# A fused attention and two-layer MLP kernel: all weight groups of the last layer converted first, their stores issued from SyncE, and one more x made on GpSimd

## The chip, the cores and the metric

One core of one Trainium2 chip runs the whole program. The time is the device time of one execution in microseconds (us); the kernel before takes 877.24 us (median of 3 runs, 876.63 to 878.43). A profile is taken of one further execution.

## The reference

Three stages follow each other. The inputs are float64 where they are weights of the two MLP layers, float32 else.

```python
phi(x): proj = x @ w_phi;  proj -= max|proj|;  return [exp(proj), exp(-proj)]
kv = phi(k)^T v;  attn = (phi(q) kv) / (phi(q) sum(phi(k)) + 1e-6)    # 4 batches x 8 heads x 576 x 64
x  = attn as 2304 tokens x 512
h  = max(max(x @ w1, x @ w2), x @ w3);  y = h @ w_out                   # d_ff 768
z  = y @ w_in;  g = max(z, 0) + alpha * min(z, 0);  out = g @ w_out2    # d_ff 2048
```

## The kernel before, in words

Two heads form a pair; the 16 pairs are worked on one after the other (line 453): queries of the pair before (`queries`, line 335) beside keys of this one (`keys`, line 267). Most products are done in three matmuls of a high and a low half (`three`, line 260).

**A pair's x.** At the end of `queries` the numerators stand in `nd[0]`; the denominators go through DRAM: `dc<-nd` (line 388), reciprocal on VectorE, `r_d<-dc` (line 393), and back, spread over partitions, as `xr<-r_d` (line 400). These DMAs are issued from GpSimd. Lines 401 to 408 then make x for each half of the 576 tokens: a product (line 402), its high half (line 405 on GpSimd, or `hi_act`, line 64, on ScalarE), and the low half, a subtraction (line 70). The choice `e` is GpSimd for the first three pairs and VectorE for all others.

**The first layer** (`layer1`, line 422) is called 48 times: 4 batches x 2 token halves x 6 groups of 128 columns. One call, a *unit* here, is 36 matmuls into three PSUM tiles `p` (line 265), which ScalarE (line 436) and VectorE (lines 437 and 439) read; GpSimd stores the result `ho` as `h_d` (line 441). Units start once batch 0 has its four x, from the fifth pair on; 14 of the 48 stand after the loop over pairs (line 623). Units of the loop share three PSUM banks, so that a bank is wanted again by the next unit.

**Weights of the later layers** come as float64 and are made into a float32 word (`words`, line 502, with `from_f64`, line 72) by two instructions on ScalarE (lines 77, 80) and two on VectorE (lines 84, 86). One such *conversion* takes a staged tile `st` (three buffers) that SyncE loads three ahead (`stage`, line 490: the next load is issued when a conversion is through), and yields a word `wt` (eight buffers). Three kinds of conversion stand in the list `todo`:
- `do_quarters` (line 529): the four column groups of `w_out2`, each 4 conversions, combined into seven words by four VectorE instructions (line 514) and *parked*, that is stored to DRAM as `q_d` (line 526), 28 stores in all; they are read back late, in the third layer (line 758).
- `do_out` (line 523): 6 conversions of `w_out`, split into high and low halves `wo`, wanted when the second layer begins (line 675).
- `do_quad` (line 555): four groups of `w_in`, each 4 conversions and 7 splits `wi`, wanted in the third stage (line 773).

That makes 38 conversions in 58 steps. After each unit behind the loop, steps are taken from the list, with low priority (line 626); in the second layer three steps after each token chunk (line 694).

**Order.** A scheduler that works with priorities and a simulated timeline writes each engine's order; engines then run in that order, and each waits in order for what it needs. So an edit in one place can change the order of hundreds of instructions elsewhere.

Of the kernel before, what the change touches and what calls it, by code (L numbers as in the profile page):

```python
# [23 lines left out]
NPAIR = H // 2  # L24
# [23 lines left out]
def tile_kernel(ctx: ExitStack, tc: tile.TileContext, qT, kT, tails, v, w_phi, w1, w2, w3, w_out, w_in, w_out2, alpha, out):  # L48
# [11 lines left out]
    nc = tc.nc  # L60
    V, A, G = nc.vector, nc.scalar, nc.gpsimd

    def hi_act(dst, src):
        A.activation(dst, src, AF.Copy)  # L64
# [4 lines left out]
    def sub(eng, dst, src, hi):  # L69
        eng.tensor_tensor(dst, src, hi.bitcast(F32), op=ALU.subtract)  # L70
# [36 lines left out]
    q_d = dram.tile([4, 7, P, 512], F32, name="q_d")  # L107

    def bank(tag, bufs, nm):
        return ps.tile([P, 512], F32, tag=tag, bufs=bufs, name=nm)  # L110
# [8 lines left out]
    def at(shape, dtype, name, tag=None, bufs=1):  # L119
        pool = ap if (tag or name) in KEYS_ONLY else lp  # L120
        return pool.tile(shape, dtype, name=name, tag=tag or name, bufs=bufs)
# [34 lines left out]
    def i_of(pair):  # L156
        return pair[0] * NPAIR + pair[1]

    def plain_kv(pair):
        return pair[0] < 2  # L160
# [57 lines left out]
    def project_queries(pair):  # L218
        ops = features(pair, "q")
        for g, tiles in enumerate(GROUPS):  # L220
            pp = at([P, 4, P], F32, tag="pp", bufs=2, name="pp")
            less_max(*project(ops, tiles), pp)
            yield g, tiles, pp
# [39 lines left out]
    def products(dst, ops, **kw):  # L263
        for i, (x, y) in enumerate(ops):
            nc.tensor.matmul(dst, x, y, start=i == 0, stop=i == len(ops) - 1, **kw)  # L265
# [69 lines left out]
    def queries(pair):  # L335

        parts = ("q",) if plain_kv(pair) else ("qh", "ql")
        qf = []
        for n, (o, w) in enumerate(CHUNKS):
            qf.append([])  # L340
            for x in parts:
                tag = f"qh{n}" if x != "ql" and pair[1] % 2 * len(x) != 1 else f"ql{n}"
                qf[n].append(at([P, 2, 2, w], F32 if plain_kv(pair) else F32R, tag=tag, bufs=1, name=x))
        nd = [at([P, S], F32, tag="nd", bufs=3, name="nd") for _ in range(2)]

        def num(n):
            o, w = CHUNKS[n]
            kv = kvs_of[pair]
            for h in range(2):
                pn = bank("p1", 3, "pn") if pair[0] == 0 else bank("pn", 1, "pn")  # L350
                ops = []
                for s in range(2):
                    q_ = [t[:, h, s] for t in qf[n]]
                    k_ = [t[:, h, s] for t in kv]
                    ops += [(k_[0], x) for x in q_] + [(x, q_[0]) for x in k_[1:]]
                products(pn[:, :w], ops)
                A.activation(nd[h][:, o : o + w], pn[:, :w], AF.Copy)

        def tail():
            yield 2, (0,), tail_of[pair]  # L360

        for g, tiles, pp in chain(project_queries(pair), tail()):
            o, w = (0, 2 * P, SM)[g], ST if g == 2 else 2 * P
            pt = bank("pn" if pair[0] == 0 and g == 1 else "pt", 1, "pt")
            for i in range(len(tiles)):
                for h in range(2):
                    c = h * len(tiles) * P + i * P
                    nc.tensor.transpose(pt[:, c : c + P], pp[:, 2 * i + h], ident)  # L368
            n = min(g, 1)
            dst = [t[:, :, :, o - CHUNKS[n][0] : o - CHUNKS[n][0] + w] for t in qf[n]]  # L370
            if plain_kv(pair):
                e = dst[0]
            else:
                e = at([P, 2, 2, 256], F32, tag="qe", bufs=2, name="qe")[:, :, :, :w]
            pv = pt[:, : 256 * len(tiles)].rearrange("p (h s) -> p h s", h=2)[:, :, -w:]
            A.activation(e[:, :, 0], pv, AF.Exp)
            A.activation(e[:, :, 1], pv, AF.Exp, scale=-1.0)
            if not plain_kv(pair):
                (hi_dve if g == 1 else hi_act)(dst[0], e)
                sub(V, dst[1], e, dst[0])  # L380
            yield
            if g != 1:
                num(n)
        yield
        dc = at([P, S // D], F32, tag="dc", bufs=2, name="dc")
        for h in range(2):
            dr = D * (1 - h)
            nc.gpsimd.dma_start(dc[h * D : (h + 1) * D], nd[h][dr : dr + 1].rearrange("a (p n) -> a p n", p=D))
        nc.gpsimd.dma_start(nd[0][D:], nd[1][D:])
        V.tensor_scalar(dc, dc, EPS, None, op0=ALU.add)  # L390
        V.reciprocal(dc, dc)
        rows = r_d[pair[0], pair[1]]
        nc.gpsimd.dma_start(rows.rearrange("h (p n) -> (h p) n", p=D), dc)
        res = []
        for c in range(2):
            cs = slice(c * CH, (c + 1) * CH)
            xr = raw_tile()
            for h in range(2):
                r = slice(h * D, (h + 1) * D)
                nc.gpsimd.dma_start(xr[r], rows[h : h + 1, cs].to_broadcast([D, CH]))  # L400
            e = G if i_of(pair) < NPAIR - 1 else V
            e.tensor_tensor(xr, nd[0][:, cs], xr, op=ALU.mult)
            xh, xl = x_tiles(c)
            if e is G:
                G.tensor_copy(xh, xr)
            else:
                hi_act(xh, xr)
            sub(e, xl, xr, xh)
            res.append((xh, xl))
        xs[pair[0]].append(res)  # L410

    def raw_tile():
        return xs_.tile([P, CH], F32, tag="xr", bufs=3, name="xr")

    def x_tiles(half):
        t = x_tile(half)
        return t[:, 0], t[:, 1]
# [65 lines left out]
    def granule(pool, nm):  # L483

        return pool.tile([P, 2, 512], F32R, tag="w", name=nm)
# [13 lines left out]
    def word():  # L499
        return sp.tile([P, 512], F32, tag="wt", bufs=8, name="wt")  # L500

    def words():

        wt = word()
        run(from_f64(staged.pop(0), wt))
        stage()
        return wt

    def split(dst, src):
        hi_act(dst[:, 0], src)  # L510
        sub(V, dst[:, 1], src, dst[:, 0])

    def both(dst, x, y, op=ALU.subtract):
        V.tensor_tensor(dst, x, y, op=op)  # L514
        return dst
# [3 lines left out]
    def split_out(k):  # L519
        wo[k] = granule(ring2, "wo")  # L520
        split(wo[k], words())

    def do_out():
        return [lambda k=k: split_out(k) for k in range(NF1)], [w_out[k] for k in range(NF1)]

    def park(p, i, x):
        nc.gpsimd.dma_start(q_d[p, i], x)

    def do_quarters(p):
        b = {}  # L530
# [24 lines left out]
    def do_quad(q):  # L555
        x = {}
        wi[q] = {}

        def get(n):
            x[n] = words()  # L560

        def to(i, n):
            pool = ring2 if (q == 0 and i < 4) or (q == 3 and i > 0) else ring
            wi[q][i] = granule(pool, "wi")
            split(wi[q][i], x[n])

        def second():
            get("22")
            x["s1"] = both(word(), x["21"], x["22"], ALU.add)

        def third():
            get("11")
            x["s2"] = both(word(), x["s1"], x["11"])
            x["s3"] = both(x["21"], x["11"], x["21"])
            to(0, "11")

        def fourth():
            get("12")
            to(1, "12")
            x["s4"] = both(x["12"], x["12"], x["s2"])  # L580

        steps = [lambda: get("21"), second, third, fourth]
        steps += [lambda i=i, n=n: to(i, n) for i, n in zip(range(2, 7), ("s2", "s1", "s3", "22", "s4"))]
        return steps, [w_in[q, a, b] for a, b in ((1, 0), (1, 1), (0, 0), (0, 1))]

    quarters = [do_quarters(p) for p in range(4)]
    for steps, src in quarters[:2] + [do_out()] + [do_quad(q) for q in range(4)] + quarters[2:]:
        todo += steps
        sources += src

# [28 lines left out]
    def convert(n):  # L619
        for _ in range(min(n, len(todo))):  # L620
            todo.pop(0)()

    for u in range(3 * (len(pairs) - NPAIR) - LAG, 12 * B):
        c, f = u // NF1 % 2, u % NF1
        layer1(u // 12, c, f, xs[u // 12], w[f], u % 2 == 0)
        with tc.high_priority(offset=LATER):
            convert(1 + u % 2)
        if u == 12 * B - NF1 - 1:
            for kk in range(NF1 // 2):
                load_h(0, kk)  # L630
            for kk in range(NF1 // 2):
                early.append(fetch_h(1, kk))
# [309 lines left out]
```

## Time and profile before

| | us |
|---|---|
| median of 3 runs | 877.24 |
| the profiled execution, its own time | 878.6 |
| its span, first to last instruction | 876.8 |
| TensorE busy | 868.5 (99%) |
| VectorE busy | 637.3 (73%) |
| ScalarE busy | 514.5 (59%) |
| GpSimd busy | 158.4 (18%) |

The granted TensorE clock is 1.00 of full speed over the span (2.4 GHz). In the rows below PE is TensorE, DVE VectorE, ACT ScalarE, POOL GpSimd, SP SyncE; a trailing q is an engine's sequencer. A row of the timeline has start, duration, engine, line, operation, what is written and read, the count of equal instructions that were merged, and in brackets the idle time of the engine before it with what ended it.

### The profile page before, as it was taken

How to read it: one execution, taken by the hardware profiler on the slowest of the kernel's cores; microseconds unless marked ns; L12 is line 12 of the kernel's file. 1: busy time of each engine (PE TensorE's matmuls, PEld its weight loads, DVE VectorE, ACT ScalarE, POOL GpSimd, SP SyncE). 2: the span in 40 equal slices, each digit the busy share in tenths (PEclk: the TensorE clock that was granted, in tenths of full speed). 3: DMA queues.
4: the chain of work that ended last, by engine and by line, in shares of the span. 5: the costliest groups of instructions: out<-in, count | busy, mean ns of one | idle time of the engine just before them, and what ended most of it. 6: DMA issues, size and time to landing. Idle time of an engine off the chain costs nothing.

```text
span 876.8 us, 17441 instructions
## 1 busy us (share of the span) xinstructions
PE 868.5 (99%) x6631; PEld 854.9 (97%) x6631; DVE 637.3 (73%) x1196; ACT 514.5 (59%) x1055; POOL 158.4 (18%) x278
## 2 busy tenths in 40 slices
PE   9999999999999999999999999999999999999998
PEld 8888899999999999999999999999999999999998
DVE  5578878877888776683965754846478899988871
ACT  4666767777677765553853554646477763544440
POOL 0354222112322244211112301111111000000000
PEclk9999999999999999999999999999999999999999
DMA  6445653223332169661688863745348746433321
GB/s 234 140 157 161 180 154 113 76 86 85 88 89 70 36 215 349 212 208 35 195 266 309 314 230 134 225 182 189 123 136 265 268 158 202 150 125 121 120 74 49
DMA packets 70436, 142.99 MB, mean 163 GB/s; under 512 B 9152, under 2 KB 36176, under 8 KB 70352
## 3 DMA queue, kind: packets, MB, share of 16 engines
q1 hardware_dynamic: 53664, 92.95, 33.2%
q0 software_dynamic: 14816, 45.26, 15.0%
q10 hardware_dynamic: 1872, 3.67, 1.2%
q8 instruction: 52, 0.85, 0.4%
q14 instruction: 32, 0.26, 0.1%
HBM read 93.07 MB, written 46.34 MB: 159 GB/s over the span
## 4 chain that ended last, share of the span: by engine, by line
PE 82%; issue 8%; DMA 4%; ACT 3%; DVE 2%; POOL 1%; POOLq 0%; DVEq 0%; ACTq 0%
PE acc L861 20%; PE p L265 16%; PE sums L773 12%; PE pj L265 6%; PE pc L773 6%; PE pn L265 6%; PE kvp L293 4%; PE p L675 3%; PE kvp L306 3%; PE pb L773 3%; DMA st<-in_w_out 2%; PE pt L368 2%; DMA xr<-r_d 1%; DVE wt L86 1%; DMA st<-in_w_in 1%
## 5 line engine op out<-in xcount | busy, mean ns | idle before, releaser
L265 PE MATMUL p<-x,w123t 128*128 128x288 f32 x1728 | 251.4, 298 | 0.4 <-ACT s L436 0.4
L265 PEld LDWEIGHTS p<-x,w123t 128*128 128x128 f32 x1728 | 235.0, 188 | 2.3 <-ACT s L436 0.8
L773 PE MATMUL sums<-x,wi 128*128 128x288 f32 x768 | 107.7, 295 | 0.0
L861 PE MATMUL acc<-wq,o 128*128 128x256 f32 x864 | 105.5, 283 | 0.0
L861 PEld LDWEIGHTS acc<-wq,o 128*128 128x128 f32 x864 | 104.2, 189 | 0.0
L773 PEld LDWEIGHTS sums<-x,wi 128*128 128x128 f32 x768 | 104.0, 188 | 0.0
L861 PE MATMUL acc<-wq,x 128*128 128x256 f32 x648 | 78.1, 280 | 0.0
L675 PE MATMUL p<-x,wo 128*128 128x288 f32 x576 | 77.0, 296 | 0.6 <-ACT yo L679 0.6
L675 PEld LDWEIGHTS p<-x,wo 128*128 128x128 f32 x576 | 76.6, 188 | 0.9 <-ACT yo L679 0.8
L861 PEld LDWEIGHTS acc<-wq,x 128*128 128x128 f32 x648 | 77.0, 188 | 0.0
L792 DVE SCALAR_TENSOR_TENSOR g<-neg,al,g 128x576 f32<-128x576 f32 x64 | 50.3, 811 | 23.6 <-ACT neg L791 23.6
L212 DVE TENSOR_REDUCE mx<-pj 128x4 f32<-128x512 f32 (+1 forms) x80 | 50.1, 628 | 12.3 <-PE pj L265 12.2
L781 ACT ACTIVATE s<-sums 128x576 f32<-128x576 f32 x48 | 31.1, 647 | 42.0 <-PE sums L773 41.9
L77 ACT ACTIVATE wt<-st 128x512 f16<-128x512 bf16 x38 | 30.1, 799 | 42.5 <-DVE wt L514 14.0
L793 POOL DMA_DIRECT2D g_d<-g x32 | 22.9, 715 | 167.2 <-DVE g L792 165.4
L441 POOL DMA_DIRECT2D h_d<-ho x48 | 28.2, 587 | 137.8 <-DVE ho L439 116.3
L245 ACT ACTIVATE ke<-pj,mx 128x128 f32<-128x128 f32 x96 | 36.9, 384 | 14.7 <-DVE mx L212 14.5
L293 PEld LDWEIGHTS kvp<-v,ke 128*128 128x128 f32 x320 | 40.6, 191 | 4.7 <-ACT kvf L318 1.8
L293 PE MATMUL kvp<-v,ke 128*128 128x128 f32 x320 | 42.9, 278 | 1.6 <-ACT kvf L318 1.6
L791 ACT ACTIVATE neg<-g 128x576 f32<-128x576 f32 x64 | 40.2, 675 | 6.3 <-DVE g L823 5.9
L64 ACT ACTIVATE o<-wt 128x512 fp32r<-128x512 f32 x45 | 27.4, 627 | 24.7 <-PE acc L861 14.2
L400 POOL DMA_DIRECT2D xr<-r_d x64 | 34.1, 539 | 32.3 <-DMA r_d<-dc 21.6
(161 smaller groups left out, 1779.6 us busy)
## 6 DMA issues: line engine op xcount, KB each, us to landing
g_d<-g POOLq DMA_DIRECT2D x32, 576.0 KB, 3.6
a<-g_d SPq DMA_DIRECT2D x36, 512.0 KB, 4.3
st<-in_w_out SPq DMA_DIRECT2D x22, 512.0 KB, 5.8
wst<-in_w SPq DMA_DIRECT2D x18, 512.0 KB, 4.0
st<-in_w_in SPq DMA_DIRECT2D x16, 512.0 KB, 4.7
yr<-y_d SPq DMA_DIRECT2D x28, 288.0 KB, 3.9
v<-in_v SPq DMA_DIRECT2D x16, 480.0 KB, 4.4
q_d<-wt POOLq DMA_DIRECT2D x28, 256.0 KB, 5.3
```

Source lines behind the costliest of these rows:

```text
L77: order(A.activation(half[:, :, 1].bitcast(F16), lanes[:, :, 3].bitcast(BF16), AF.Copy))
L212: V.tensor_reduce(mx, pv, axis=AX.X, op=ALU.max, apply_absolute_value=True, negate=True)
L245: A.activation(ev[:, a, 0], pv[:, a], AF.Exp, bias=mx[:, a : a + 1])
L265: nc.tensor.matmul(dst, x, y, start=i == 0, stop=i == len(ops) - 1, **kw)
L293: nc.tensor.matmul(kvp[:, j * P : (j + 1) * P], e[:, c], rv[:, t, j // 2 : j // 2 + 2].rearrange("p a d -> p (a d)"), start=first, stop=t ...
L400: nc.gpsimd.dma_start(xr[r], rows[h : h + 1, cs].to_broadcast([D, CH]))
L675: nc.tensor.matmul(p2[m // 2][1][:, m % 2], x, y, start=k + n == 0, stop=k == NF1 - 1 and n == 2)
L773: nc.tensor.matmul(dst[:, j], a, b, start=start and n == 0, stop=n == len(ops) - 1, skip_group_check=True)
L781: A.activation(s, src, AF.Copy)
L791: A.activation(neg, gv[:, j], AF.Relu, scale=-1.0)
L792: V.scalar_tensor_tensor(gv[:, j], neg, al[:, f + j : f + j + 1], gv[:, j], op0=ALU.mult, op1=ALU.add)
L861: nc.tensor.matmul(acc[i], x, y, start=half == 0 and f == 0 and n == 0 and place[i][1] == 0, stop=half == 1 and f == 3 and n == 2, skip_gr ...
```

## The change

Four lines. The x of the fourth pair is made by GpSimd like those of the first three. The parked words are stored from SyncE. All four `do_quarters` stand first in the list, then `do_out`, then the quads. After each unit behind the loop two steps are taken, where it was one and two in turn.

```diff
-            e = G if i_of(pair) < NPAIR - 1 else V
+            e = G if i_of(pair) < NPAIR else V
...
-        nc.gpsimd.dma_start(q_d[p, i], x)
+        nc.sync.dma_start(q_d[p, i], x)
...
-    for steps, src in quarters[:2] + [do_out()] + [do_quad(q) for q in range(4)] + quarters[2:]:
+    for steps, src in quarters + [do_out()] + [do_quad(q) for q in range(4)]:
...
-            convert(1 + u % 2)
+            convert(2)
```

The first place is GpSimd's order around the fourth pair's x (`xr` is the spread reciprocal and then the product, `x` its halves, `nd` the numerators).

```order
 L393 DMA r_d<-dc 128x9
 L400 DMA xr<-r_d 64x288 x4
-L388 DMA dc<-nd 64x1x9 x2
+L402 TENSOR_TENSOR xr<-nd,xr 128x288
+L388 DMA dc<-nd 64x1x9
+L405 CAST x<-xr 128x288
+L402 TENSOR_TENSOR xr<-nd,xr 128x288
+L70 TENSOR_TENSOR x<-xr,x 128x288
+L405 CAST x<-xr 128x288
+L388 DMA dc<-nd 64x1x9
 L389 DMA nd<-nd 64x576
+L70 TENSOR_TENSOR x<-xr,x 128x288
```

Six instructions come to GpSimd behind the loads of `xr`. The four that they replace on VectorE (lines 402 and 70, twice each) and the two on ScalarE (line 64) are gone there.

The second place is TensorE's order at the same time: the first unit's matmuls with the fourth pair's x (`p_803`, `p_816`, `p_829`), the next pair's key products (`kvp`) and projections (`pj`), and transposes of the pair's features (`pt`). Before:

```order
L265 MATMUL pn<-q,kvf 128x320 x2
L265 MATMUL p_803<-x,w123t 128x288
L265 MATMUL p_816<-x,w123t 128x288
L265 MATMUL p_829<-x,w123t 128x288
L265 MATMUL p_803<-x,w123t 128x288 x2
L265 MATMUL p_816<-x,w123t 128x288 x2
L265 MATMUL p_829<-x,w123t 128x288 x2
L293 MATMUL kvp<-v,ke 128x128 x7
```

Changed:

```order
L265 MATMUL p_829<-x,w123t 128x288
L265 MATMUL pj<-wph,xhk 128x256
L265 MATMUL pj<-wpl,xhk 128x256
L265 MATMUL pj<-wph,xlk 128x256
L265 MATMUL pj<-wph,xhk 128x256
L265 MATMUL pj<-wpl,xhk 128x256
L265 MATMUL pj<-wph,xlk 128x256
L265 MATMUL pj<-wph,xht 128x256
L265 MATMUL pj<-wpl,xht 128x256
L265 MATMUL pj<-wph,xlt 128x256
L368 MATMUL pt<-ident,pp 128x128 x4
L265 MATMUL p_803<-x,w123t 128x288 x2
```

Nine projections and four transposes move between the matmuls that need the high half of x and those that need the low half, and so ahead of the key products.

The third place is SyncE's queue where the conversions begin (`st` is the staged weight group, `q_d` the parked words).

```order
-L493 DMA st<-in_w_out 128x1024 x14
-L493 DMA st<-in_w_in 128x1024 x5
+L493 DMA st<-in_w_out 128x1024 x5
+L527 DMA q_d<-wt 128x512 x2
+L493 DMA st<-in_w_out 128x1024
+L527 DMA q_d<-wt 128x512 x3
+L493 DMA st<-in_w_out 128x1024
+L527 DMA q_d<-wt 128x512 x2
+L493 DMA st<-in_w_out 128x1024 x2
+L527 DMA q_d<-wt 128x512 x2
+L493 DMA st<-in_w_out 128x1024
+L527 DMA q_d<-wt 128x512 x3
```

A store stands between two loads there now, two or three times in a row; the pattern goes on until 28 stores are issued. On GpSimd the 28 rows of line 527 are gone.

## Rows read from the trace of the kernel before

**Rows 1.** The page's first part: busy us, share, instructions of each engine.
```profile
PE 868.5 (99%) x6631; PEld 854.9 (97%) x6631; DVE 637.3 (73%) x1196; ACT 514.5 (59%) x1055; POOL 158.4 (18%) x278
```

**Rows 2.** TensorE's waits, all but one: us in total, times, longest.
```profile
PE kvp L293 <- ACT kvf L318: 1.6, 1, 1.6
PE warm L130 <- DVE signs L132: 1.1, 1, 1.1
PE p L675 <- ACT yo L679: 0.6, 1, 0.6
...
PE pn L265 <- ACT q L376: 0.5, 1, 0.5
PE p L265 <- ACT s L436: 0.4, 1, 0.4
```

**Rows 3.** TensorE's timeline at the first wait.
```profile
87.28 1.59 PE L265 MATMUL p<-x,w123t 128*128 128x288 f32 x9
90.45 1.83 PE L293 MATMUL kvp<-v,ke 128*128 128x128 f32 x14 [1.57 <-ACT kvf L318]
```

**Rows 4.** The chain of waits: a run of 12 matmuls (start, us).
```profile
516.76 1.59 PE pb L773 x12
```

**Rows 5.** VectorE's and ScalarE's timelines ahead of the first wait.
```profile
85.86 0.46 DVE L402 TENSOR_TENSOR xr<-nd,xr 128x288 f32<-128x288 f32 x1 [1.73 <-DMA xr<-r_d]
86.23 0.68 DVE L212 TENSOR_REDUCE mx<-pj 128x4 f32<-128x512 f32 x1
90.00 0.68 DVE L216 TENSOR_TENSOR pp<-pj,mx 128x512 f32<-128x512 f32 x1
...
89.74 0.66 ACT L318 ACTIVATE kvf<-kvp 128x512 f32<-128x512 f32 x1
```

**Rows 6.** GpSimd's timeline, third pair; line 405 (ns min/median/max).
```profile
70.47 0.80 POOL L402 TENSOR_TENSOR xr<-nd,xr 128x288 f32<-128x288 f32 x1
71.23 0.80 POOL L70 TENSOR_TENSOR x<-xr,x 128x288 fp32r<-128x288 f32 x1
85.08 0.52 POOL L388 DMA_DIRECT2D dc<-nd  x1 [0.44 <-ACT nd L357]
L405 POOL CAST x<-xr x6: 424/546/958, 41.0 to 72.0; 128x288 fp32r<-128x288 f32 x6
```

**Rows 7.** VectorE beside GpSimd's third pair; line 84; the window's busy times.
```profile
69.97 2.40 DVE L84 TENSOR_SCALAR wt<-wst 128x512 uint16<-128x512 uint16 x1
...
L84 DVE TENSOR_SCALAR wt<-wst x18: 444/460/2401, 18.0 to 151.4; 128x512 uint16<-128x512 uint16 x18
...
50.00:75.00 25.00, 25.00 (x168) 22.71 (x167) 20.06 (x40) 18.33 (x52) 16.63 (x27) 1.00 0.51 160
```

**Rows 8.** Timelines at TensorE's wait in the first layer.
```profile
373.85 4.36 PE L265 MATMUL p<-x,w123t 128*128 128x288 f32 x31 [0.40 <-ACT s L436]
...
367.91 0.45 ACT L64 ACTIVATE x<-xr 128x288 fp32r<-128x288 f32 x1 [5.14 <-DVE xr L402]
...
367.42 0.46 DVE L402 TENSOR_TENSOR xr<-nd,xr 128x288 f32<-128x288 f32 x1 [2.95 <-DMA xr<-r_d]
```

**Rows 9.** Timelines at TensorE's wait in the second layer.
```profile
484.01 0.80 ACT L77 ACTIVATE wt<-st 128x512 f16<-128x512 bf16 x1 [5.11 <-issue]
...
487.02 5.18 PE L675 MATMUL p<-x,wo 128*128 128x288 f32 x37 [0.61 <-ACT yo L679]
```

**Rows 10.** Windows: length, busy PE PEld DVE ACT POOL, clock, DMA share, GB/s.
```profile
320.00:340.00 20.00, 20.00 (x153) 20.00 (x153) 16.86 (x37) 12.18 (x25) 12.72 (x23) 1.00 0.91 307
340.00:360.00 20.00, 19.97 (x148) 19.58 (x148) 11.46 (x27) 11.51 (x19) 5.65 (x11) 1.00 0.87 306
360.00:375.00 15.00, 14.61 (x110) 14.37 (x109) 9.59 (x21) 7.64 (x16) 4.26 (x8) 1.00 0.63 192
```

**Rows 11.** DMA issues: count, KB each, median us from issue to landing.
```profile
st<-in_w_out SPq DMA_DIRECT2D x22, 512.0 KB, 5.8
...
q_d<-wt POOLq DMA_DIRECT2D x28, 256.0 KB, 5.3
```

## The prediction

> **What bounds the kernel now.** The page's first part comes first: TensorE is busy for 868.5 us of a span of 876.8 [rows 1]. The changed kernel issues the same matmuls, so no engine's relief is worth anything by itself; all that can be won is TensorE's idle time and all that can be lost is new idle time. The next view is therefore who TensorE waited for [rows 2]. There are six waits in all, each once, together under 5 us. The one on VectorE's `signs` is the start of the program and stays. Three lie in stretches that the change rewrites: 1.6 us for the copy `kvf`, 0.4 us for ScalarE's read of a first-layer tile, 0.6 us for ScalarE's read of a second-layer tile. Their places are found in the timeline [rows 3, 8, 9], at 90.45, 373.85 and 487.02 us. The windows last: while weights are converted, the DMA engines are busy for 0.91 and 0.87 of the time at 307 and 306 GB/s [rows 10]. That is the one resource near its limit which the change loads more.
>
> **The fourth pair's x (82 to 93 us).** Before, TensorE begins nine matmuls at 87.28 and the next one at 90.45 [rows 3]. Twelve take 1.59 us in the steady third stage [rows 4], that is 0.133 each, so nine are worth 1.20 and 1.97 us are lost. The copy `kvf` is late (89.74) because ScalarE's exponentials ahead of it want a maximum that VectorE reduces at 86.23, and VectorE stood idle for 1.73 us until 85.86 for the landing of `xr` [rows 5]. In the new order VectorE has no instruction there that waits for `xr`, so that reduction can start 1.73 us before 85.86, at 84.1. `kvf` comes earlier by as much, TensorE reaches the key products later, behind nine projections and four transposes, and this wait is gone: -1.97.
>
> Two waits can take its place. First, the three matmuls at 87.28 need the high half from GpSimd. `xr` lands at 85.86 as before; then product 0.80, the issue of `dc` that stands between, 0.52, cast 0.55 [rows 6]: 87.73. That is 0.45 late; with the shortest and the longest cast it is 0.3 and 0.9.
>
> Second, the four transposes need `pp`, the last of nine instructions that begin with that reduction. Before, the stretch from 86.23 to the end of `pp` at 90.68 [rows 5] held those nine and three of the moved ones (some 0.37 each, from start to start), so the nine take 4.45 - 1.1 = 3.35 and `pp` is ready at 84.1 + 3.35 = 87.5 if nothing slows them. TensorE comes to the transposes after twelve matmuls, 1.6 us at most, so at 89.3. But GpSimd now works beside them. With the third pair, VectorE's shift of line 84 lasted 2.40 us beside GpSimd's product and subtraction at 70.47 and 71.23, where its median is 0.46 [rows 6, 7]. The same shift stands in this chain. Its excess, 1.94, puts `pp` at 89.4 or, since the reduction also has to wait for its projection, up to 0.4 later: a wait of 0.1 to 0.5, and I take 0.4. The bounds: none if nothing is blocked; if VectorE stood still for all of GpSimd's six instructions (four of 0.80, two of up to 0.96, 5.1 us), `pp` is ready at 92.6 and the wait is 3.3. I stay near the measured shift, since in the window 50 to 75, where the third pair's x is made on GpSimd, TensorE is busy for 25.00 of 25.00 us [rows 7]. The low halves are ready at 87.73 + 2 x 0.80 = 89.3, when TensorE is not yet there. This part: -1.97 + 0.45 + 0.4 = -1.1, between -1.7 and +2.2.
>
> The Trainium skill ("SBUF — State Buffer", section "SBUF: two separate sides") says that VectorE and GpSimd share one pair of ports which is locked for a whole instruction, against a VectorE instruction in a two-port mode or with two SBUF inputs, and that the loser waits to the end. The trace agrees: 2.40 us against 0.46 [rows 7]. By the rule at its worst this part would be the +2.2 above, and the whole change no gain, which is how this speaks against moving work from VectorE to GpSimd.
>
> **The first layer's end (310 to 437 us).** At 373.85 TensorE waited 0.40 for ScalarE, which had stood 5.14 us at the cast of the last pair's x; VectorE's product was waiting for the landing of `xr` [rows 8]. In the new order that cast stands after the tile read of the next unit (`p_4752`) and not ahead of it, one unit of 36 matmuls, 4.8 us, later. So -0.4; 0 if `xr` lands 4.8 us later than now.
>
> What is added here is conversions: 36 of the 38 stand ahead of the end of the first layer, where it was 28, and 14 stores more. Their instructions, two each on ScalarE and VectorE, fall on engines busy for 7.6 to 17 us of 15 to 20 [rows 10]; TensorE feels them only if a tile read is queued behind a conversion whose load is late. Loads of 512 KB landed in 5.8 us, stores of 256 KB in 5.3 [rows 11]. On SyncE a load now stands behind two or three stores, each waiting for its VectorE instruction; but every load is wanted three conversions later, and that covers it. On GpSimd the 28 issues vanish, which only helps `xr` and `h_d`. I cost queues and instructions at 0. The DMA engines are a rival.
>
> **The second layer.** At 484.01 ScalarE had stood 5.11 us at a conversion, a tile read was queued behind it, and TensorE waited 0.61 [rows 9]. Ten conversions and fourteen stores stood in this layer; two conversions and no store are left. -0.6; at worst 0, as one of the two could still stall.
>
> **Sum.** -1.1 - 0.4 - 0.6 = -2.1. The profiled execution took 878.6 us in all, 1.8 more than its span, so 876.5 by its own measure. It lies 1.4 above the median of the runs; taken from that, 877.24 - 2.1 = 875.1.
>
> **Rivals.**
> - *DMA engines late, slower.* By the new order 17 conversions stand ahead of the last read of the 32nd unit (`ho` of `p_4778`, at some 373 us), where it was 16; and with the quarters first, 14 more stores. That is one load and 14 stores more, 0.52 + 14 x 0.262 = 4.2 MB. At 307/0.91 = 337 GB/s for all 16 engines, the free share from 320 to 373 (20 x 0.09 + 20 x 0.13 + 13 x 0.37 = 9.2 us) [rows 10] carries 3.1 MB; 1.1 MB are left over, a lag of 3.3 us. The bank of that read is wanted 38 matmuls, 5.0 us, after its last matmul, so the lag is covered. If instead 307 GB/s is all they do, only the last 13 us have room, 13 x (307 - 192) = 1.5 MB; 2.7 MB are left, a lag of 8.8 and a stall of 3.8. With the early and the late gain (-1.1 - 0.6) this ends at 879.3. For it: both windows stand at the same 306 to 307. Against: ScalarE was busy for only 12 of 20 us there and TensorE lost nothing to it, so conversions already ran late without harm. It decides from a lag above 5.0 us.
> - *No change.* The lock takes the early gain whole (0 for that part), and the new order, which differs on every engine from 90 us on, has a small new wait of half a microsecond; -0.4 - 0.6 + 0.5 = -0.5, so 876.7. For it: the scheduler's simulated timeline does not know the lock. Against: the two later waits lose their cause.
> - *All waits go.* No new one appears early: -1.97 - 0.4 - 0.6 = -3.0, so 874.3. Against: GpSimd's cast cannot be ready at 87.28.
> - *The change does not do what it says*: conversions could be pushed late by their low priority. The order excludes this (36 of 38).
>
> **How the numbers follow.** My forecast 0.40, all waits go 0.10, no change 0.29, DMA engines late 0.21. The bound for no change is 0.2%, 1.75 us, about what a measurement of this kernel can tell. The forecast lies 0.35 beyond it, so a tenth of its chance falls inside: faster 0.47, same 0.32, slower 0.21. Low end: 874.3 less 1.0, since waits under the trace's notice may go too: 873.3. High end: the slow rival's 879.3 and a little, 879.6. Without that rival the range is 873.3 to 877.2.
>
> **What would show it.** In the changed profile: no wait for `kvf` near 90 us, but one of some 0.45 before the first `p` with the fourth pair's x, whose releaser is GpSimd; a shift of line 84 or a subtraction on VectorE of over 1.5 us near 88; no wait of TensorE at the last pair's x nor in the second layer. DMA share above 0.9 from 320 to 375, ScalarE standing at line 77 for loads, and TensorE without idle time there. I am wrong if TensorE waits there for line 436 or 439, or if waits appear between 100 and 310 us, where none of the six lies now.

## The result

The changed kernel is slower: 883.77 us, median of 5 runs (882.66 to 885.74), against 877.24 us (876.09 to 879.85) for the kernel before on the same chip; ratio 1.0069, 95% interval 1.0046 to 1.0091, some 6 us. The forecast was 875.1 us, and the time lies outside its range. The profiled execution took 883.5 us with a span of 881.7 (before: 878.6 and 876.8).

**The profile after.** The page's first part: busy us, share, instructions of each engine [rows 1].

```profile
PE 870.6 (99%) x6631; PEld 855.8 (97%) x6631; DVE 640.4 (73%) x1192; ACT 516.2 (59%) x1053; POOL 146.3 (17%) x256
```

The same 6631 matmuls. Of the 4.9 us that the span is longer, 2.8 are idle time of TensorE (881.7 - 870.6 against 876.8 - 868.5), and for 2.1 it is counted busy longer. (The medians lie 6.5 us apart; the profiled execution before took 1.4 us more than its median.) TensorE's waits, all but three (us in total, times, longest) [rows 2]:

```profile
PE kvp L293 <- ACT ke L245: 3.1, 2, 2.8
PE pj L265 <- DVE pp L216: 1.5, 1, 1.5
...
PE pj L265 <- DVE my L243: 0.4, 1, 0.4
PE pj L265 <- DVE ppt L216: 0.3, 1, 0.3
```

The waits for `kvf`, for `yo` and for `s` of line 436 are gone, as forecast. In their place stands a wait of 2.8 us for the key exponentials, which no step of the forecast had, and one of 1.5 us for `pp`, which had 0.4. The windows place them (length, busy PE PEld DVE ACT POOL, clock, DMA share, GB/s):

```profile
85.00:100.00 15.00, 13.32 (x99) 12.13 (x98) 13.81 (x30) 11.79 (x34) 7.07 (x12) 1.00 0.58 174
100.00:150.00 50.00, 46.15 (x329) 43.11 (x328) 36.60 (x91) 31.31 (x81) 10.89 (x20) 1.00 0.51 138
300.00:400.00 100.00, 99.88 (x761) 99.46 (x760) 76.38 (x154) 65.16 (x128) 23.07 (x41) 1.00 0.75 260
475.00:500.00 25.00, 25.00 (x190) 25.00 (x189) 8.77 (x12) 7.92 (x13) 2.17 (x4) 1.00 0.58 179
```

The kernel before:

```profile
85.00:100.00 15.00, 13.43 (x99) 12.62 (x97) 11.95 (x34) 12.05 (x33) 2.70 (x6) 1.00 0.63 179
100.00:150.00 50.00, 50.00 (x366) 47.67 (x365) 39.83 (x99) 34.30 (x89) 14.17 (x25) 1.00 0.49 145
300.00:400.00 100.00, 99.58 (x754) 98.94 (x753) 70.30 (x146) 58.10 (x116) 29.52 (x53) 1.00 0.65 219
475.00:500.00 25.00, 24.39 (x182) 24.05 (x182) 15.94 (x26) 12.81 (x22) 5.94 (x11) 1.00 0.91 328
```

Length less busy PE is the idle time. It is all but unchanged at 85 to 100 us (1.57, now 1.68), falls in the last two (0.42 to 0.12, 0.61 to 0), and at 100 to 150, where TensorE had none, it is 3.85 us. The loss lies there: TensorE has 329 matmuls in that window where it had 366, and 37 at 0.133 us are 4.9 us, an estimate, since their sizes differ. So a part of the time that counts as busy is lost there too. In the last two windows it has 7 and 8 matmuls more than before.

**The chain behind the 2.8 us.** Timelines of the changed kernel, in order of time: ScalarE reads the sixth pair's sum (`nd`, line 357), GpSimd issues the small transfer `dc<-nd`, VectorE adds the constant to `dc` (line 390) and behind that reduces the next key projections (line 212), ScalarE takes their exponentials (line 245), TensorE multiplies them.

```profile
111.89 0.45 ACT L357 ACTIVATE nd<-pn 128x320 f32<-128x320 f32 x1
113.61 0.54 POOL L388 DMA_DIRECT2D dc<-nd  x1 [1.76 <-ACT q L377]
119.27 0.17 DVE L390 TENSOR_SCALAR dc<-dc 128x9 f32<-128x9 f32 x1 [4.01 <-DMA dc<-nd]
120.02 1.28 DVE L212 TENSOR_REDUCE mx<-pj 128x4 f32<-128x512 f32 x2
121.33 0.37 ACT L245 ACTIVATE ke<-pj,mx 128x128 f32<-128x128 f32 x1 [5.93 <-DVE mx L212]
121.75 0.49 PE L293 MATMUL kvp<-v,ke 128*128 128x128 f32 x2 [2.78 <-ACT ke L245]
```

The same links in the kernel before:

```profile
107.98 0.44 ACT L357 ACTIVATE nd<-pn 128x320 f32<-128x320 f32 x1 [0.61 <-PE pn L265]
109.69 0.54 POOL L388 DMA_DIRECT2D dc<-nd  x1 [1.37 <-ACT ke L245]
114.04 0.17 DVE L390 TENSOR_SCALAR dc<-dc 128x9 f32<-128x9 f32 x1 [3.03 <-DMA dc<-nd]
115.27 0.69 DVE L212 TENSOR_REDUCE mx<-pj 128x4 f32<-128x512 f32 x1
119.94 0.37 ACT L245 ACTIVATE ke<-pj,mx 128x128 f32<-128x128 f32 x1
120.64 0.38 PE L293 MATMUL kvp<-v,ke 128*128 128x128 f32 x2
```

VectorE stood at line 390 ahead of the reductions there too, for 3.03 us, and TensorE lost nothing by it: the exponential was through at 120.31 and wanted at 120.64, 0.33 us later. In the new order TensorE begins the four products for this `nd` at 108.23 (before: 106.70), and ScalarE reads them behind seven exponentials of the key projection, two casts and a conversion and not ahead of them, 3.9 us later in all; the chain is later by that and by a transfer that takes 1.3 us longer from issue to line 390 (5.66 against 4.35). No instruction of the edit stands in it.

### The profile page after: what moved, and what is told of

The parts are those of the page before. It is cut to its first block, busy times and chain, and to the rows that moved or that the text cites. A ratio compares the mean times of both kernels' runs of the same rounds, so it can differ in the third digit from the quotient of the medians.

```text
span 881.7 us, 17419 instructions
## 1 busy us (share of the span) xinstructions
PE 870.6 (99%) x6631; PEld 855.8 (97%) x6631; DVE 640.4 (73%) x1192; ACT 516.2 (59%) x1053; POOL 146.3 (17%) x256
## 4 chain that ended last, share of the span: by engine, by line
PE 83%; DMA 1%; issue 0%; DVE 0%; POOL 0%; ACT 0%; DVEq 0%
PE p L265 23%; PE acc L861 20%; PE sums L773 12%; PE p L675 9%; PE pc L773 6%; PE pn L265 3%; PE kvp L306 3%; PE pj L265 3%; PE pb L773 3%; PE pt L368 1%; DMA st<-in_w_out 1%; DMA xr<-r_d 1%; PE kvt L325 0%; POOL xr L400 0%; DVE s L437 0%
```

## The experiments

All ratios are to the kernel before on the same chip, whose median was 876.8 to 877.3 us each time. The table collects the times and TensorE's idle time by stretch, from the windows of one profile each. Experiments 2, 6 and 7 run in the order of before up to some 315 us, and their profiles differ from it by up to 0.8 us at 85 to 100 and 0.4 us at 100 to 150; differences of that size in these columns show little. Nor does idle time hold what a lower clock costs.

| kernel | ratio, 95% interval | 85-100 | 100-150 | 300-400 | 475-500 |
|---|---|---|---|---|---|
| before | 1 | 1.57 | 0 | 0.42 | 0.61 |
| changed | 1.0069 (1.0046 to 1.0091) | 1.68 | 3.85 | 0.12 | 0 |
| x on GpSimd only | 1.0124 (1.0088 to 1.0160) | 1.00 | 3.44 | 2.41 | 0 |
| change without the x edit | 1.0013 (0.9996 to 1.0031) | 1.32 | 0 | 1.94 | 0 |
| changed, five `nd` | 1.0078 (1.0050 to 1.0106) | 1.04 | 2.93 | 0.28 | 0 |
| the same, addition behind | 1.0036 (1.0018 to 1.0053) | 1.15 | 0.54 | 0.25 | 0 |
| changed, GpSimd cut short | 1.0050 (1.0031 to 1.0069) | 0 | 1.89 | 2.49 | 0 |
| stores from SyncE only | 1.0023 (1.0008 to 1.0038) | 1.25 | 0.44 | 2.34 | 0 |
| groups first, two a unit | 1.0081 (1.0064 to 1.0098) | 0.80 | 0.20 | 5.25 | 0 |
| casts on VectorE | 1.0044 (1.0027 to 1.0061) | 0.48 | 1.58 | 0.88 | 0 |
| casts on VectorE, and the rest | 1.0016 (1.0005 to 1.0027) | 1.86 | 0.79 | 0 | 0 |
| before, five `nd` | 1.0083 (1.0057 to 1.0110) | 0.73 | 4.43 | 0.18 | 0 |
| before, four `xr` | 1.0049 (1.0027 to 1.0072) | 1.30 | 0 | 3.06 | 0 |
| before, other priority | 1.0030 (1.0017 to 1.0043) | 1.50 | 0 | 2.08 | 0 |

**1. The x edit alone.** Up to 300 us its order is that of the changed kernel.

```diff
-            e = G if i_of(pair) < NPAIR - 1 else V
+            e = G if i_of(pair) < NPAIR else V
```

> Only the fourth pair's x goes to GpSimd; groups, conversions and stores stay as before. My theory: all of the loss comes from this edit, through the order that follows from it (the two traces show 0.6 us at 85 to 91 us and 5.0 us between 105 and 135 us), and the other three edits give about 1.5 us back, so this kernel is slower than the changed one: 885.3 us (884.3 to 886.3), with the 2.8 us wait of TensorE for the key exponentials near 121 us. Rival (the loss is in the last layer's groups and stores): about 876 us, without that wait.

888.69 us (886.27 to 889.87). The loss comes with this edit: the wait near 121 us is there (2.3 us), and the rival's 876 is far off. It is 3 us slower than I expected, and that is in a place I had not thought of: 300 to 400 us, where new waits (1.6 us for `nd`, 0.5 for `s`, 0.4 for line 437) came with yet another order. The granted clock was 0.98 there and 0.97 at 100 to 150 (changed: 1.00); 0.02 of 100 us is some 2 us more that the table does not show, an estimate. So "the other three edits give 1.5 us back" is wrong as a sum; what they give depends on the order they meet.

**2. The change without the x edit.** Its order is that of before up to 300 us.

```diff
-            e = G if i_of(pair) < NPAIR else V
+            e = G if i_of(pair) < NPAIR - 1 else V
```

> The change without its edit of the fourth pair's x: groups first, two conversions a unit, stores from SP. My theory: the first 300 us are those of the kernel before, with the 1.6 us wait for kvf; the waits for the eviction of yo (0.6 us) and for s at the end of the first layer (0.4 us) are gone; 875.7 us (875.0 to 876.5), faster than both. Rival (the loss is in the last layer's groups and stores): 881 to 883 us.

878.76 us (876.25 to 881.15): no difference that can be told from before, neither my 875.7 nor the rival's 881 to 883. 100 to 150 us is clean, and the waits for `yo` and `s` are gone. But a new wait of 1.9 us takes their gain. VectorE's timeline, and the matmul that waited for it:

```profile
339.02 0.47 DVE L84 TENSOR_SCALAR wt<-st 128x512 uint16<-128x512 uint16 x1 [1.59 <-DMA st<-in_w_out]
340.53 0.69 DVE L86 TENSOR_TENSOR wt<-wt,st 128x512 uint32<-128x512 uint32 x1 [0.71 <-ACT st L80]
341.14 0.45 DVE L439 TENSOR_TENSOR ho<-p,s 128x288 f32<-128x288 f32 x1
...
341.65 36.55 PE L265 MATMUL p<-x,w123t 128*128 128x288 f32 x262 [1.94 <-DVE ho L439]
```

A conversion waits for its load, and the tile read `ho` is queued behind it. This is the mechanism of my slow rival.

**3 and 4. The addition ahead of the reductions.** To take it out of the way without another change ahead of it, the sixth pair's addition is written a pair later and given a key maximum as second operand (a negative number, so the result stays). That needs more `nd` buffers, hence the control with five.

```diff
-        nd = [at([P, S], F32, tag="nd", bufs=3, name="nd") for _ in range(2)]
+        nd = [at([P, S], F32, tag="nd", bufs=5, name="nd") for _ in range(2)]
...
-        V.tensor_scalar(dc, dc, EPS, None, op0=ALU.add)
+            V.tensor_scalar(dc, dc, begun['mx'][:, :1], EPS, op0=ALU.max, op1=ALU.add)
```

> The changed kernel with five buffers for nd in place of three; a control for the next one. From 70 us on the order of every engine is that of the changed kernel. Theory and rival alike: the 2.8 us wait for the key exponentials near 121 us stays, 883.8 us (882.8 to 884.8); below 883 only if the earlier order gains something.

> The kernel with five buffers for nd, in which the sixth pair's addition to dc, and what follows from it, is written later and reads a key maximum (the result stays the same): in VectorE's order it now stands behind the two key reductions in place of ahead of them. Up to there the order is the same, from there on not. My theory (the addition's wait for a small transfer holds up the reductions, these the exponentials, these TensorE): the 2.8 us wait near 121 us falls below 0.5 us and TensorE is busy over 24 of the 25 us from 100 to 125; the whole is 2 to 3 us shorter, 881.0 us (879 to 882.5), as far as the later order adds no wait. Rival (the exponentials are late because VectorE or ScalarE have too much to do there): the wait stays within 1 us of 2.8 and the time within 1 us of the kernel with five buffers.

885.43 us (881.62 to 887.21) for the control, whose order is that of the changed kernel from 93 us on and whose wait was 1.6 us and not 2.8, and 881.27 (878.43 to 882.66) with the addition behind. VectorE's timeline and the window, first the control, then the other (its line 402 is the addition):

```profile
117.37 0.17 DVE L390 TENSOR_SCALAR dc<-dc 128x9 f32<-128x9 f32 x1 [2.90 <-DMA dc<-nd]
118.12 1.28 DVE L212 TENSOR_REDUCE mx<-pj 128x4 f32<-128x512 f32 x2
...
100.00:150.00 50.00, 47.07 (x340) 44.43 (x339) 37.69 (x94) 31.53 (x82) 9.67 (x18) 1.00 0.46 137
```

```profile
116.72 1.28 DVE L212 TENSOR_REDUCE mx<-pj 128x4 f32<-128x512 f32 x2
120.73 0.23 DVE L402 TENSOR_SCALAR dc<-dc,mx 128x9 f32<-128x9 f32 x1
...
100.00:150.00 50.00, 49.46 (x355) 46.71 (x354) 38.34 (x95) 32.69 (x83) 11.05 (x20) 1.00 0.46 139
```

The reductions no longer stand behind the transfer, the wait near 121 us is gone, and the idle time of the stretch falls from 2.93 to 0.54 us. By medians the kernel is faster by 4.2 us, more than I gave it; the two profiled executions, 882.1 and 881.3 us, differ by 0.8 only, so how much of the 4.2 is this wait stays open. From the addition to TensorE's wait the chain is shown, and the rival refuted; why the transfer came later in the changed kernel is read from the timelines alone. The order changes from there on, and a wait of 1.2 us for `nd` at 158 us takes a part back.

**5. GpSimd's six operations cut short.** 32 columns in place of 288, and the others set to zero ahead, so that a part of the result is left out; VectorE's order is the same up to 91 us.

```diff
+            W = 32 if i_of(pair) == 3 else CH
-            e.tensor_tensor(xr, nd[0][:, cs], xr, op=ALU.mult)
+            e.tensor_tensor(xr[:, :W], nd[0][:, cs][:, :W], xr[:, :W], op=ALU.mult)
```

> The changed kernel with GpSimd's product, cast and difference of the fourth pair cut from 288 to 32 columns each (the other columns of that x are left at zero, so this part of the computation is left out). VectorE's order is that of the changed kernel up to the cast at 91 us, from there on it is another one; so only 84 to 92 us is read. My theory (GpSimd's six operations stretch VectorE's beside them): VectorE's cast of q goes from 1.03 to about 0.42 us, the difference xlq from 2.19 to about 0.7, and TensorE's wait for pp near 91 us from 1.5 us to below 0.5. Rival (VectorE's own queue is too long there, whoever makes x): the wait stays above 1.0 us.

882.02 us (878.46 to 883.80). VectorE's cast, subtraction and `pp`, two of GpSimd's operations beside them, and the matmul that waited, in the changed kernel:

```profile
86.24 1.03 DVE L67 CAST xhq<-q 128x512 fp32r<-128x512 f32 x1 [0.18 <-PE pj L265]
87.80 2.19 DVE L70 TENSOR_TENSOR xlq<-q,xhq 128x512 fp32r<-128x512 f32 x1
90.49 0.67 DVE L216 TENSOR_TENSOR pp<-pj,mx 128x512 f32<-128x512 f32 x1
...
86.20 0.79 POOL L402 TENSOR_TENSOR xr<-nd,xr 128x288 f32<-128x288 f32 x1 [1.20 <-DMA xr<-r_d]
88.63 0.80 POOL L70 TENSOR_TENSOR x<-xr,x 128x288 fp32r<-128x288 f32 x1
...
91.31 0.36 PE L265 MATMUL pj<-wph,xht 128*128 128x256 f32 x1 [1.49 <-DVE pp L216]
```

The same with 32 columns, and its window (in this kernel the lines from 388 on lie 5 or 6 further down):

```profile
85.51 0.43 DVE L67 CAST xhq<-q 128x512 fp32r<-128x512 f32 x1 [0.18 <-PE pj L265]
86.45 0.68 DVE L70 TENSOR_TENSOR xlq<-q,xhq 128x512 fp32r<-128x512 f32 x1
87.46 0.67 DVE L216 TENSOR_TENSOR pp<-pj,mx 128x512 f32<-128x512 f32 x1
...
85.12 0.25 POOL L408 TENSOR_TENSOR xr<-nd,xr 128x32 f32<-128x32 f32 x1 [1.14 <-DMA xr<-r_d]
...
85.00:100.00 15.00, 15.00 (x116) 14.48 (x116) 12.17 (x33) 12.50 (x35) 5.95 (x13) 1.00 0.62 182
```

From the start of the cast to `pp` it is 4.25 us beside GpSimd's full operations and 1.95 without; the wait is gone and TensorE is busy for 15.00 of 15.00 us. TensorE has six first-layer matmuls (0.8 us) more ahead of the projections here, but the one that waited begins at 89.08, 0.95 us after the end of `pp`, so the wait would be gone without them too. So the edit does what it is meant to do (before had 1.57 us of idle time here), and GpSimd's slowing of VectorE takes all of it back. The wait near 120 us came here too (1.9 us; VectorE stood 4.14 us at the addition, ahead of the reductions), in an order that differs once more.

**6 and 7. The other edits one by one.**

```diff
-        nc.gpsimd.dma_start(q_d[p, i], x)
+        nc.sync.dma_start(q_d[p, i], x)
```

> The kernel before with the stores of the converted groups issued from SP and nothing else. Theory A (a load of the next weights stands behind a store that waits for its conversion, so the loads come later and VectorE waits for them with the first layer's maxima behind that wait): a new wait of TensorE of 0.5 to 2 us between 320 and 375 us, 877.5 to 880 us. Theory B (the stores are harmless there, the added conversions fill the DMA engines): within 0.7 us of the kernel before.

```diff
-    for steps, src in quarters[:2] + [do_out()] + [do_quad(q) for q in range(4)] + quarters[2:]:
+    for steps, src in quarters + [do_out()] + [do_quad(q) for q in range(4)]:
...
-            convert(1 + u % 2)
+            convert(2)
```

> The kernel before with the groups first and two conversions in every unit, stores still from GpSimd. Theory A (the loads behind stores on SP make the wait): the waits for yo at 487 us and for s at 374 us go, no new one comes, 875.7 to 876.5 us. Theory B (the added conversions fill the DMA engines): the wait of about 2 us for ho near 340 us is here too, 877.5 to 880 us.

879.12 us (876.50 to 883.92) and 884.70 us (881.68 to 886.12). Stores from SyncE alone: waits for `ho` of 1.4 and 0.9 us, and the wait for `yo` gone; within theory A. Groups first without them: neither theory's number, and both failed by size; the waits come later, at 376 to 392 us. The last pair's `xr` reads stand behind the stores in GpSimd's queue: they go out at 368.87 (before at 362.05, in the changed kernel at 363.83). But that is not what TensorE waits for. The last of them goes out at 370.83 and is through within 6.6 us, by 377.5; VectorE takes up its product only at 384.15, behind a conversion that waits for its load. VectorE's timeline and one of TensorE's waits:

```profile
378.00 0.46 DVE L84 TENSOR_SCALAR wt<-st 128x512 uint16<-128x512 uint16 x1 [1.78 <-DMA st<-in_w_out]
378.35 0.45 DVE L439 TENSOR_TENSOR ho<-p,s 128x288 f32<-128x288 f32 x1
...
383.79 0.47 DVE L84 TENSOR_SCALAR wt<-st 128x512 uint16<-128x512 uint16 x1 [0.55 <-DMA st<-in_w_in]
384.15 0.44 DVE L402 TENSOR_TENSOR xr<-nd,xr 128x288 f32<-128x288 f32 x1
...
385.64 0.53 PE L265 MATMUL p<-x,w123t 128*128 128x288 f32 x2 [1.03 <-ACT x L64]
```

So the two waits for x (1.0 and 0.2 us) and the two for `ho` (3.1 us) all stand behind late loads, as in experiment 2; why the loads are late here stays open. Each alone costs; with both, the idle time at 300 to 400 us was 0.12 us in the changed kernel and none in experiment 9, but 1.94 in experiment 2.

**8 and 9. The same relief without GpSimd.**

```diff
-                hi_act(xh, xr)
+                (hi_dve if i_of(pair) == NPAIR - 1 else hi_act)(xh, xr)
```

> The kernel before with one line changed: the two casts of the fourth pair's x go from ScalarE to VectorE, GpSimd has no part in it. In the order that follows, VectorE's addition to dc of the sixth pair stands behind the two key reductions. My theory (the wait for kvf came from the casts in ScalarE's queue, GpSimd's work took its gain away again by slowing VectorE, and the wait near 120 us comes from the addition ahead of the reductions): no wait for kvf, less than 0.5 us of wait for the key exponentials near 120 us, TensorE's excess from 75 to 100 us down from 3.7 to 1.0 to 2.2 us, 875.2 us (874.2 to 876.5). Rival (any edit here costs several us in the order after 100 us): 878 to 883 us, with waits of 1.5 us or more between 105 and 135 us.

> The same two casts on VectorE, with the other three edits of the change (groups first, two conversions a unit, stores from SP). Theory A (the three edits are worth their 1.3 us when the first 300 us hold no new wait): 874.2 us (873.2 to 875.5), faster than with the casts alone. Theory B (at 325 to 375 us they bring VectorE a wait for weights that costs what they give): 0 to 3 us slower than with the casts alone, with a wait of TensorE for ho or s there.

879.91 us (878.38 to 884.04) and 878.50 us (876.68 to 880.28). My number for the first was wrong by almost 5 us, and the rival's is nearer, though its waits of 1.5 us are not there either. What the theory named happened: no wait for `kvf`, none near 120 us, 0.48 us idle at 85 to 100. Several small new waits stand in their place, 0.7 us at 108 (`ke`), 0.8 at 133 (`ppt`), 0.7 at 347 (`s`). But in all TensorE is idle for 8.1 us, as before (8.3), so this profile does not show where the 2.9 us by medians come from. The second is 1.4 us faster than the first by medians and without idle time from 300 us on, theory A in sign, but its level is wrong with the first's: it has two waits for the key exponentials (3.4 us together, at 74 and 92 us). Up to some 315 us the two kernels run in the same order, and the first's profile has 0.5 us of this wait; the rest is a difference between two executions of one order.

**10 to 12. Another order and nothing else.** Three edits that move no work.

```diff
-        nd = [at([P, S], F32, tag="nd", bufs=3, name="nd") for _ in range(2)]
+        nd = [at([P, S], F32, tag="nd", bufs=5, name="nd") for _ in range(2)]
```

```diff
-        return xs_.tile([P, CH], F32, tag="xr", bufs=3, name="xr")
+        return xs_.tile([P, CH], F32, tag="xr", bufs=4, name="xr")
```

```diff
-SOON, NOW, LATER, LAST = 400, 1000, -100, -200
+SOON, NOW, LATER, LAST = 400, 1000, -140, -200
```

> The kernel before with five buffers for nd in place of three: no work is added, moved or taken away, but the order of TensorE, VectorE and ScalarE is another one from about 50 us on. Theory A (the order by itself is worth microseconds, and the one of before is a good one): 878 to 884 us, with new waits of TensorE for VectorE or ScalarE between 50 and 150 us of together 2 us or more. Theory B (the order matters only where an edit adds work): within 0.8 us of the kernel before.

> The kernel before with four buffers for xr in place of three: the same instructions, another order from about 180 us on. Theory A (the order by itself is worth microseconds): 878 to 882 us, with new waits of TensorE between 300 and 400 us, where ScalarE and VectorE also convert weights; from 180 to 300 us less, since the attention has its exponentials well ahead there. Theory B: within 0.8 us of the kernel before.

> The kernel before with the queries' and conversions' priority at -140 in place of -100: the same instructions, another order from about 200 us on. Theory A: 878 to 882 us, with new waits of TensorE between 300 and 400 us. Theory B: within 0.8 us of the kernel before.

882.53 us (881.67 to 886.10), 879.83 (877.70 to 886.76) and 879.58 (877.70 to 879.78): all three slower, theory A. The first has two waits for ScalarE's read of `nd`, 1.85 us at 109 and 1.81 at 122; in the last, VectorE stands for a load ahead of a tile read, though TensorE loses only 0.34 us by that one:

```profile
349.62 0.47 DVE L84 TENSOR_SCALAR wt<-st 128x512 uint16<-128x512 uint16 x1 [3.46 <-DMA st<-in_w_out]
349.98 0.43 DVE L437 TENSOR_TENSOR s<-p,s 128x288 f32<-128x288 f32 x1
```

No version tried beats the kernel before.

## Why the prediction was wrong

- **The fourth pair's x, -1.1: wrong in size.** The wait for `kvf` went, and experiment 5 shows the -1.97 to be near the truth (1.57 us of idle time gone). The 0.45 for three matmuls that wait for GpSimd did not come. The wait for `pp`, 0.4 in the sum, measured 1.49. The stretch was hardly what was mis-sized: the cast and the subtraction took 0.60 and 1.51 us more than in experiment 5, 2.1 together, against the 1.94 taken from the third pair's one shift [rows 7]. (That shift was not alone in the trace before: the subtraction `xlq` behind it, at 72.85, took 1.69 us, where experiment 5 has 0.68.) But the chain began at 84.99, not at 84.1 to 84.5, and unslowed it takes 3.87 us (from 84.26 to 88.13 in experiment 5), not the 3.35 that I had worked out; each is half a microsecond, and the slack that they used up was all that stood before the wait. TensorE also needed `pp` earlier than worked out: not at the transposes but three matmuls ahead of them, at the seventh projection, whose tile `pp` reads. Read from the idle time, this part is +0.1. By the rule of the Trainium skill ("SBUF — State Buffer", section "SBUF: two separate sides") at its worst, VectorE would have stood for all of GpSimd's six operations, 5.1 us by the prediction's estimate. The trace agrees with the rule that VectorE waits, by the two instructions it stretches, and not with the worst case: it is 2.1 us, beside 3.7 us of GpSimd's operations from 86.20 to the end of `pp`.
- **The order after 93 us: the step that failed.** The sum had no term for it; only the rival of no change had "a small new wait of half a microsecond". It measured 3.85 us of idle time at 100 to 150, 2.8 of them in one chain: key reductions behind an addition that waits for a small transfer. Experiment 4 shows that link, and experiments 1 and 2 that the wait came with the x edit. I had read the order at three places on which a term rested, and none of them lies there. The trace before held the warning: VectorE stood 3.03 us for a small transfer with the key reductions behind it, and TensorE was spared only because the next exponentials were 0.33 us early. A list of TensorE's waits shows what is late now, not what is nearly late.
- **The first layer's end, -0.4, and the second layer, -0.6: the numbers came, the reasons are not shown.** The idle time fell by 0.30 and 0.61 us. But experiments 1, 2, 6 and 7 show that the first is no property of the edits: alone or in other company that stretch has 1.9 to 5.3 us of idle time. The second was luck as far as these runs go: its wait is gone in every other kernel of the table too, also in the six that leave the list of conversions as it was (experiments 1, 6, 8, 10, 11 and 12). In experiment 6 ScalarE stood even longer at a conversion, with a tile read behind it, and TensorE had no idle time there:

```profile
483.03 0.81 ACT L77 ACTIVATE wt<-st 128x512 f16<-128x512 bf16 x1 [5.72 <-DMA q_d<-wt]
```

- **The DMA rival (879.3): did not decide.** The DMA share was as high as it said, and TensorE was busy throughout:

```profile
352.00:372.00 20.00, 20.00 (x152) 20.00 (x152) 14.05 (x31) 10.20 (x18) 6.22 (x11) 1.00 1.03 382
```

  The 337 GB/s that I took for all that the engines do was too low. Its mechanism, a tile read behind a conversion whose load is late, is real in experiment 2, not in the changed kernel.
- **The chances.** 0.21 for slower, all of it for the DMA rival, was too little: I took a place without a wait for a place with slack. The sign "I am wrong if waits appear between 100 and 310 us" named it.

## What to carry to other kernels

Where a scheduler writes the order, an edit is priced in two parts: what it moves, and a draw of a new order behind it; here three edits that move no work cost 0.3 to 0.8%, so the second part was larger than the first and needs a term of its own. Look for its size before: every place where an engine stands for a transfer with urgent work queued behind it, even if nobody waits now, can become a loss of microseconds in another order. That nearly every order tried here was slower suggests that the one before was a good one; how often a draw loses elsewhere is not shown. And work moved to GpSimd beside VectorE's 128x512 casts and subtractions was charged to VectorE here: add the stretch of each of these that stands on the way to TensorE.

## What the runs showed of the hardware

- Beside GpSimd's 128x288 operations a 128x512 cast on VectorE took 1.03 us in place of 0.43 and a subtraction 2.19 in place of 0.68 (experiment 5).
- After some waits of about 2 us TensorE's granted clock fell for a few microseconds, to 0.50, the 1.2 GHz level, in one window. With the x edit alone, the wait of 2.29 us ended at 120.64:

```profile
120.00:122.00 2.00, 1.36 (x8) 1.36 (x9) 2.00 (x6) 0.48 (x2) 0.46 (x1) 0.86 0.00 0
122.00:124.00 2.00, 2.00 (x10) 2.00 (x10) 2.00 (x6) 2.00 (x6) 0.12 (x1) 0.50 0.61 154
124.00:128.00 4.00, 4.00 (x33) 4.00 (x32) 3.15 (x10) 3.13 (x9) 2.64 (x5) 0.89 0.94 239
```

  By these shares that is 0.28 + 1.00 + 0.44 = 1.7 us more, an estimate, nearly as much as the wait. The same followed the 1.94 us wait of experiment 2 (0.72 and 0.86 in its two windows of 4 us). It did not follow the 2.78 us wait of the changed kernel, nor the two of 1.85 and 1.81 us in experiment 10, which all stayed at 1.00; what tells them apart stays open.
- The DMA engines moved 382 GB/s at a share of 1.03 (352 to 372 us of the changed kernel).
